# The third batch's attention scores from q and k as loaded (float32), and the order of the whole program searched anew

## The chip, the cores and the metric

The kernel runs on one core of one Trainium2 chip. The metric is the device time of the whole program in microseconds (us), the median of several runs. TensorE (PE in the rows) has the matrix products, VectorE (DVE), ScalarE (ACT) and GpSimd (POOL) the work by element, and SyncE (SP) issues every transfer from one queue, in order.

## The reference

```python
B, H, S, D = 8, 8, 576, 64                       # batches, heads, tokens, width of a head
scores = matmul(q, k.T) / sqrt(D)
cum = cumsum(log(clip(f, 1e-4, 1)), axis=-1)
scores = where(causal, -1e9, scores + cum[:, :, :, None] - cum[:, :, None, :])
attn = softmax(scores)
x = matmul(attn, v)                              # [8 * 576, 512] after the heads are put side by side
h = x @ w_in                                     # [4608, 1024]
solu = h * softmax(h)
ln = (solu - mean(solu)) / sqrt(var(solu) + 1e-6) * g_ln
out = ln @ w_out                                 # [4608, 512]
```

Here q and k are of such a size that rounding them once to 16 bits is too coarse for the result.

## The kernel before

**Attention.** Two heads of a batch make a pair: 32 pairs, four to a batch, pairs 0 to 3 in batch 0. Within a pair the 576 queries are cut into five row blocks, of which block i sees 64 + 128i keys (64, 192, 320, 448 and 576; the last in two pieces of 288). For each piece `score_products` multiplies q by k for both heads, one head on each half of the array's rows (L825), and adds the decay by a product with `pick` or `e8` (L823, L821). VectorE then takes the mask and the row maximum (L846), ScalarE the exponential with its sum (L851), GpSimd and VectorE the reciprocal (L857, L858). The weights of a row block are written as two float16 words (high by ScalarE or GpSimd through the helper lines L507 and L509, low by VectorE, L879), turned by a transposing DMA (L516), and multiplied by v (L928).

**Two ways to the scores.** `NAT` says for how many batches q and k are used as they were loaded. For pairs of batches 0 to NAT - 1, `load` brings q and k straight into one of the four slots `qk16_0` to `qk16_3` (in the rows qk, qk_0_70 to qk_3_73), and L825 is one float32 product for each piece and head. A float32 product is recorded as two weight loads and two matmuls. For the other batches `load` brings them into one of four buffers `raws`. ScalarE then sums their squares (`squares`, L687), a chain of small VectorE and TensorE steps turns the sums into powers of two (`scale`, L640 to L676), and `split_qk` writes each of q and k as a high word (GpSimd, L509) and a low word (VectorE, L780) into the slot. L825 is then three float16 products: high by high, low by high, high by low. v is split in the same way for all batches but the first, so that its squares and its scale exist for every batch.

**The layer.** The 4608 tokens are 36 layers of 128 tokens. Each takes 24 products of 512 columns with w_in (L959 to L961, two words on both sides), the maximum (L970), the exponential (L973), products and sums (L977, L987), the normalisation (L997), two words of the result (L507, L1001), a transposing DMA, and 24 products with w_out (L1029 to L1031). A layer starts when the four pairs of its tokens are done, while later pairs are still under way.

**The order.** Every step is an `op` of a planner, `Plan`. It places the steps on the five engines by a greedy rule, in which the number that a step has in the table `RANK` decides among those that could go next. The engines then run the lists that come out of it, each strictly in its order. `NAT` alters the number of steps (a batch taken as loaded has no squares, no scale and no words of q and k), so that a table belongs to one NAT.

**Filler products.** Where the planner expects TensorE to be idle in the first 300 us, products of `ident` with itself are put into its list (L1154), so that its clock is not lowered. Their number follows from the planner's expectation. Their output is never read.

Of the kernel before, what the change touches and what calls it, by code (L numbers as in the profile page):

```python
# [48 lines left out]
NRAW, NQK, NS, NAT = 4, 4, 6, 2  # L49
# [31 lines left out]
class Plan:  # L81
# [159 lines left out]
    1, 10, 5, 18, 27, 2, 4, 3, 15, 25, 6, 16, 20, 8, 24, 30, 32, 36, 39, 41, 31, 33, 38, 42, 46, 49, 85, 167, 171, 182, 163, 185, 34, 126, 12, 14, 21,  # L241
    28, 7, 22, 11, 40, 9, 29, 13, 56, 59, 62, 67, 72, 77, 17, 97, 90, 105, 109, 114, 127, 132, 143, 23, 26, 35, 44, 48, 177, 191, 47, 55, 58, 64, 70,
    60, 63, 69, 73, 78, 82, 84, 92, 96, 98, 94, 65, 71, 68, 76, 80, 54, 89, 86, 100, 118, 103, 112, 93, 110, 95, 119, 116, 121, 133, 149, 155, 37, 45,
    52, 57, 74, 138, 157, 75, 83, 104, 108, 101, 106, 124, 123, 120, 115, 129, 131, 140, 137, 142, 134, 99, 0, 107, 102, 111, 125, 117, 122, 145, 147,
    141, 159, 139, 144, 130, 136, 169, 172, 175, 184, 188, 50, 66, 79, 87, 91, 195, 206, 113, 151, 150, 146, 148, 153, 154, 156, 158, 161, 165, 168,
    197, 170, 199, 180, 162, 166, 176, 173, 179, 181, 183, 187, 204, 245, 189, 211, 192, 194, 196, 205, 248, 250, 260, 270, 273, 51, 81, 88, 128, 135,
    164, 174, 160, 178, 210, 200, 212, 198, 217, 220, 214, 202, 223, 225, 239, 246, 254, 243, 203, 201, 207, 209, 213, 218, 227, 224, 258, 261, 253,
    262, 233, 256, 234, 237, 263, 267, 269, 277, 279, 190, 230, 216, 240, 296, 259, 193, 247, 231, 257, 272, 265, 244, 278, 382, 390, 293, 300, 266,
    289, 291, 298, 302, 306, 314, 318, 322, 335, 340, 343, 370, 383, 359, 365, 388, 446, 379, 451, 381, 445, 403, 452, 395, 469, 353, 467, 347, 283,
    288, 290, 292, 294, 297, 303, 308, 315, 323, 330, 339, 356, 374, 392, 408, 419, 430, 402, 424, 444, 440, 443, 453, 457, 472, 477, 494, 517, 524,  # L250
    531, 338, 351, 355, 366, 372, 377, 380, 386, 393, 404, 413, 423, 428, 435, 441, 460, 455, 476, 463, 470, 479, 482, 485, 501, 503, 508, 521, 537,
    539, 615, 625, 208, 221, 219, 215, 226, 222, 251, 255, 264, 268, 228, 235, 232, 236, 242, 241, 249, 252, 271, 275, 276, 421, 274, 396, 282, 418,
    280, 407, 286, 400, 320, 325, 334, 341, 238, 299, 281, 284, 285, 287, 295, 313, 319, 316, 304, 309, 307, 311, 317, 321, 326, 329, 333, 331, 324,
    327, 332, 362, 348, 354, 345, 350, 342, 357, 411, 416, 427, 439, 312, 360, 344, 337, 352, 346, 358, 361, 363, 368, 369, 376, 373, 378, 384, 391,
    399, 405, 409, 414, 398, 420, 397, 425, 438, 437, 429, 433, 426, 436, 431, 442, 449, 458, 389, 447, 410, 406, 415, 412, 422, 434, 461, 450, 456,
    462, 459, 465, 468, 475, 483, 490, 493, 506, 471, 474, 480, 492, 528, 526, 448, 515, 514, 520, 549, 565, 579, 581, 590, 597, 599, 603, 611, 632,
    641, 645, 652, 662, 673, 688, 691, 703, 713, 737, 743, 756, 726, 734, 739, 786, 792, 796, 800, 805, 806, 808, 812, 817, 819, 684, 690, 700, 705,
    720, 742, 746, 751, 765, 778, 788, 799, 797, 809, 824, 833, 840, 854, 901, 904, 974, 909, 911, 917, 920, 954, 1028, 967, 229, 305, 367, 454, 301,
    364, 336, 371, 385, 387, 394, 401, 473, 484, 432, 545, 466, 498, 481, 486, 488, 496, 491, 495, 499, 500, 504, 510, 512, 519, 516, 522, 535, 530,
    527, 525, 507, 505, 513, 509, 518, 523, 529, 533, 542, 536, 546, 534, 547, 582, 584, 586, 596, 602, 532, 543, 538, 540, 541, 544, 548, 550, 552,  # L260
    555, 573, 560, 553, 558, 551, 556, 562, 559, 569, 572, 577, 583, 598, 594, 606, 604, 655, 665, 674, 721, 417, 502, 557, 561, 564, 578, 563, 566,
    585, 587, 568, 571, 591, 607, 610, 616, 612, 614, 618, 623, 620, 621, 567, 570, 574, 580, 589, 592, 601, 605, 608, 613, 622, 631, 638, 675, 678,
    694, 706, 709, 576, 617, 593, 588, 600, 595, 609, 619, 624, 627, 630, 637, 633, 642, 629, 636, 654, 649, 657, 667, 679, 671, 699, 683, 663, 729,
    762, 769, 785, 813, 464, 497, 628, 635, 639, 650, 640, 647, 664, 666, 656, 670, 677, 681, 686, 701, 685, 687, 693, 704, 689, 695, 644, 646, 660,
    658, 668, 682, 702, 708, 692, 712, 696, 714, 724, 775, 777, 779, 791, 801, 648, 710, 669, 659, 676, 680, 697, 707, 718, 715, 753, 750, 717, 723,
    719, 725, 727, 759, 757, 787, 793, 790, 807, 804, 770, 811, 828, 844, 888, 892, 478, 511, 716, 731, 732, 736, 730, 733, 741, 755, 738, 747, 760,
    764, 767, 789, 766, 772, 784, 795, 774, 781, 748, 744, 752, 749, 758, 763, 773, 768, 780, 776, 794, 802, 783, 821, 822, 823, 829, 834, 754, 816,
    798, 810, 803, 814, 835, 845, 848, 851, 853, 857, 827, 832, 825, 830, 837, 842, 871, 890, 893, 902, 907, 910, 864, 914, 965, 972, 1007, 1011, 152,
    489, 349, 487, 839, 855, 859, 862, 867, 870, 878, 883, 898, 906, 912, 922, 923, 929, 941, 950, 962, 973, 1030, 1033, 1038, 1046, 1050, 1120, 1127,
    1145, 1160, 1164, 925, 928, 930, 935, 939, 945, 948, 951, 959, 968, 976, 986, 988, 998, 1025, 1032, 1040, 1051, 1100, 1105, 1110, 1126, 1149,  # L270
    1151, 1174, 1179, 1187, 1193, 985, 990, 997, 1005, 1012, 1014, 1017, 1020, 1029, 1036, 1047, 1062, 1054, 1085, 1129, 1152, 1172, 1184, 1218, 1225,
    1108, 1230, 1242, 1248, 1255, 1264, 1271, 1279, 1055, 1059, 1065, 1072, 1075, 1078, 1082, 1087, 1095, 1102, 1121, 1135, 1128, 1142, 1161, 1169,
    1220, 1231, 1273, 1286, 1292, 1297, 1307, 1320, 1336, 1341, 1349, 1382, 1137, 1141, 1162, 1166, 1182, 1186, 1204, 1206, 1221, 1224, 1238, 1252,
    1247, 1269, 1284, 1301, 1331, 1353, 1409, 1412, 1420, 1423, 1428, 1431, 1433, 1443, 1448, 1452, 43, 61, 53, 19, 575, 186, 328, 634, 310, 375, 643,
    651, 653, 661, 672, 698, 885, 897, 728, 820, 745, 818, 761, 949, 979, 836, 882, 841, 846, 849, 850, 863, 856, 858, 869, 872, 894, 891, 874, 877,
    896, 895, 886, 880, 843, 847, 860, 866, 881, 889, 980, 899, 937, 952, 1042, 900, 955, 963, 964, 983, 1016, 1026, 852, 969, 868, 873, 875, 887,
    903, 908, 916, 919, 957, 977, 924, 931, 921, 926, 936, 915, 960, 970, 981, 978, 994, 1018, 987, 1023, 1093, 1097, 1101, 1103, 771, 876, 722, 815,
    782, 1015, 933, 958, 942, 944, 943, 946, 956, 961, 947, 953, 984, 989, 996, 999, 1004, 1000, 993, 1001, 1003, 1006, 966, 971, 1009, 1019, 1031,
    1037, 1064, 1048, 1077, 1071, 1021, 1013, 1081, 1111, 1113, 1115, 1117, 1125, 992, 1024, 1008, 1002, 1034, 1027, 1049, 1056, 1061, 1057, 1119,
    1092, 1035, 1039, 1041, 1044, 1045, 1060, 1098, 1099, 1107, 1122, 1148, 1150, 1124, 1155, 1188, 1194, 1203, 1254, 740, 861, 735, 838, 913, 1022,  # L280
    1043, 1053, 1066, 1068, 1063, 1067, 1073, 1074, 1076, 1079, 1104, 1106, 1118, 1114, 1112, 1116, 1133, 1083, 1130, 1132, 1086, 1091, 1090, 1096,
    1139, 1144, 1156, 1158, 1159, 1183, 1146, 1136, 1196, 1235, 1237, 1240, 1244, 1250, 1131, 1153, 1140, 1138, 1157, 1143, 1168, 1173, 1185, 1201,
    1189, 1215, 1165, 1170, 1163, 1167, 1175, 1181, 1207, 1213, 1233, 1243, 1263, 1259, 1222, 1267, 1268, 1313, 1323, 1344, 831, 927, 865, 934, 1010,
    1080, 1171, 1200, 1177, 1180, 1176, 1178, 1195, 1197, 1190, 1192, 1202, 1214, 1216, 1226, 1217, 1223, 1256, 1228, 1227, 1246, 1208, 1210, 1211,
    1219, 1232, 1245, 1265, 1260, 1280, 1283, 1261, 1251, 1288, 1325, 1328, 1330, 1338, 1342, 1212, 1258, 1229, 1234, 1236, 1241, 1249, 1253, 1262,
    1257, 1303, 1266, 1270, 1274, 1272, 1276, 1277, 1281, 1294, 1300, 1358, 1310, 1367, 1348, 1306, 1387, 1456, 1461, 1494, 1497, 1346, 1357, 1363,
# [912 lines left out]
```

## Time and profile before

| | us |
|---|---|
| median of 3 runs | 665.16 (665.11 to 666.92) |
| the profiled execution, its own time | 663.76 |
| its span, from the first to the last instruction | 661.9 |
| TensorE busy in it | 633.3 |
| VectorE busy in it | 558.0 |
| ScalarE busy in it | 519.7 |
| GpSimd busy in it | 403.0 |

The span lies within the execution's own time; 1.9 us are outside. The own time is 1.4 us under the median. "Busy" is the time in which an engine has at least one instruction under way. Matmuls overlap and their ends are modelled, so the distance from one start to the next says more than a duration. An idle time carries the name of what ended it. A wait for several things is put down to the one that came last. The mean granted TensorE clock was 0.997 of its full 2.4 GHz.

### The profile page before, as it was taken

What the parts mean: (1) busy time and instruction counts of PE and PEld (TensorE: products, weight loads), DVE (VectorE), ACT (ScalarE), POOL (GpSimd) and SP (SyncE); (2) the same over time, 40 slices, a digit from 0 to 9 for tenths busy, and PEclk for the clock granted to TensorE, in tenths of its full rate; (3) what the DMA queues carried; (4) which work ended last, traced back from release to release, by engine and by line L of the source; (5) the groups of instructions that cost most, each with busy time, mean ns of one, the idle gap of its engine ahead of it and who ended that gap; (6) DMA issues with size and microseconds to landing.
All of it is one profiled execution on the core that took longest, in us unless ns stands there. A gap on an engine that the chain in (4) does not pass through costs nothing. (4 is left out here: it accounts for less than half of the span.)

```text
span 661.9 us, 17333 instructions
## 1 busy us (share of the span) xinstructions
PE 633.3 (96%) x6304; PEld 343.2 (52%) x6304; DVE 558.0 (84%) x1640; ACT 519.7 (79%) x1294; POOL 403.0 (61%) x625
## 2 busy tenths in 40 slices
PE   6899999999999999999999999999998999999998
PEld 4655655655554546454454555445544544544445
DVE  6777999999998999999989998889899977884222
ACT  6999938978979989898796996998786869655432
POOL 4465851386767845887578666765776645556440
PEclk9999999999999999999999999999999999999999
DMA  8856118879889997999899898699657984877341
GB/s 340 315 187 227 41 37 231 143 128 225 173 174 191 189 213 145 170 246 202 197 166 197 157 226 201 151 195 190 136 117 136 156 155 83 160 133 141 78 96 48
DMA packets 262709, 110.79 MB, mean 167 GB/s; under 512 B 248288, under 2 KB 248736, under 8 KB 261600
## 3 DMA queue, kind: packets, MB, share of 16 engines
q1 hardware_dynamic: 262624, 109.69, 77.1%
q8 instruction: 49, 0.80, 0.5%
q14 instruction: 36, 0.29, 0.1%
HBM read 38.27 MB, written 9.66 MB: 72 GB/s over the span
## 5 line engine op out<-in xcount | busy, mean ns | idle before, releaser
L851 ACT ACTIVATE p<-p,nm 128x448 f32<-128x448 f32 (+4 forms) x208 | 132.9, 641 | 25.7 <-DVE nm L846 25.3
L825 PE MATMUL ps<-qk 64*128 64x288 f16 (+9 forms) x1056 | 103.3, 306 | 8.6 <-DMA qk<-in_qk_dram 4.9
L959 PE MATMUL hps<-wi_h,x_h 128*128 128x512 f16 x288 | 109.6, 381 | 1.8 <-DVE e L977 1.8
L961 PE MATMUL hps<-wi_h,x_l 128*128 128x512 f16 x288 | 109.1, 379 | 0.0
L960 PE MATMUL hps<-wi_l,x_h 128*128 128x512 f16 x288 | 109.1, 379 | 0.0
L1029 PE MATMUL ps<-wo_f,zz 128*128 128x512 f16 x280 | 106.6, 381 | 2.4 <-DVE p16s L879 1.3
L857 POOL TENSOR_SCALAR sm<-sm 128x2 f32<-128x2 f32 (+1 forms) x128 | 38.5, 301 | 111.7 <-ACT p L851 83.1
L1031 PE MATMUL ps<-wo_f,zz 128*128 128x512 f16 x280 | 106.1, 379 | 0.0
L1030 PE MATMUL ps<-wo_f,zz 128*128 128x512 f16 x280 | 106.1, 379 | 0.0
L846 DVE CUSTOM_DVE_ANT_0 p<-ps,mask 128x448 f32<-128x448 f32 (+4 forms) x208 | 97.6, 497 | 5.8 <-PE ps L823 3.0
L879 DVE SCALAR_TENSOR_TENSOR wo_p<-p,ri,wo_p 128x448 f16<-128x448 f32 (+1 forms) x112 | 96.5, 880 | 3.7 <-ACT wo_p L507 2.6
L1001 POOL TENSOR_TENSOR z<-e,z 128x1024 f16<-128x1024 f32 x32 | 71.6, 2239 | 21.6 <-ACT z L507 21.2
L928 PE MATMUL ps<-t_p,v 128*64 128x128 f16 (+1 forms) x2520 | 80.7, 219 | 3.1 <-DVE nm L846 1.5
L928 PEld LDWEIGHTS <-v 128*64 128x64 f16 x2520 | 70.8, 110 | 24.7 <-issue 22.6
L970 DVE TENSOR_REDUCE st<-hps 128x1 f32<-128x1024 f32 x36 | 43.7, 1214 | 28.6 <-PE hps L961 28.6
L509 POOL TENSOR_SCALAR wo_p<-p,ri 128x576 f16<-128x576 f32 x56 | 52.9, 952 | 14.9 <-DVE ri L858 10.1
L973 ACT ACTIVATE e<-hps,st,unscale 128x1024 f32<-128x1024 f32 x32 | 38.4, 1201 | 25.0 <-DVE st L971 19.9
L823 PE MATMUL ps<-crow,pick 64*128 64x448 bf16 (+1 forms) x360 | 51.7, 276 | 0.0
L977 DVE SCALAR_TENSOR_TENSOR e<-hps,e 128x1024 f32<-128x1024 f32 x36 | 43.8, 1217 | 9.3 <-ACT e L973 8.8
L825 PEld LDWEIGHTS <-qk 64*128 64x128 f16 x864 | 32.3, 94 | 37.0 <-issue 26.1
L997 POOL TENSOR_SCALAR e<-e,st 128x1024 f32<-128x1024 f32 x32 | 47.4, 1483 | 2.9
L509 POOL TENSOR_SCALAR qk<-raws,scale 128x576 f16<-128x576 f32 x48 | 40.3, 844 | 14.6 <-DVE scale L676 8.3
(188 smaller groups left out, 1300.4 us busy)
## 6 DMA issues: line engine op xcount, KB each, us to landing
raws<-in_qk_dram SPq DMA_DIRECT2D x24, 576.0 KB, 4.8
vraw<-in_v_dram SPq DMA_DIRECT2D x8, 1280.0 KB, 6.7
out_dram<-y SPq DMA_DIRECT2D x35, 256.0 KB, 2.8
qk<-in_qk_dram SPq DMA_DIRECT2D x8, 576.0 KB, 7.9
wo_raw<-in_w_in_dram SPq DMA_DIRECT2D x4, 1024.0 KB, 7.9
t_raw<-in_w_out_dram SPq DMA_DIRECT2D x2, 1024.0 KB, 4.8
vraw<-in_w_out_dram SPq DMA_DIRECT2D x2, 1024.0 KB, 6.2
t_p<-p16s SPq DMA_TRANSPOSE x84, 3.4
```

Of the source, the lines that this page charges most:

```text
L509: (nc.vector if eng == DVE else nc.gpsimd).tensor_scalar(now(out_), now(in_), scale, by, ALU.mult, ALU.mult)
L825: nc.tensor.matmul(dst, x[row(h), 0, q0:q0 + P], y[row(h), 1, cols], start=(n == 0), stop=False)
L846: op(DVE, R_NS[i] if n == 0 else 442, at[i][h] + STEPS[0], lambda i=i, h=h, n=n, a=a, e=e, x=x, m0=m0: nc.vector.tensor_tensor_reduce(home ...
L851: op(ACT, E_NS[i] + (0 if banked(p, i) or i == 4 else 28), at[i][h] + STEPS[1], lambda i=i, h=h, x=x: nc.scalar.activation(home(i, h), hom ...
L879: op(DVE, L_NS[j], at[j][g] + STEPS[4], lambda j=j, g=g, nq=nq, h16=h16, l16=l16, r1=r1: nc.vector.scalar_tensor_tensor(l16(), home(j, g, ...
L928: nc.tensor.matmul(o[row(h), a:a + n], v16[m][:, x, 2 * j + h], t[:, y, i + j if h else i - j], start=(j == 0 and c == 0), stop=(j == i an ...
L959: nc.tensor.matmul(hps[:, sl], x_h, wi_h[:, c, sl], start=(c == 0), stop=False)
L960: nc.tensor.matmul(hps[:, sl], x_h, wi_l[:, c, sl], start=False, stop=False)
L961: nc.tensor.matmul(hps[:, sl], x_l, wi_h[:, c, sl], start=False, stop=(c == NCC - 1))
L1029: nc.tensor.matmul(o, zz[:, a, 0, j], wo(0, k), start=(k == 0), stop=False)
L1030: nc.tensor.matmul(o, zz[:, a, 0, j], wo(1, k), start=False, stop=False)
L1031: nc.tensor.matmul(o, zz[:, a, 1, j], wo(0, k), start=False, stop=(k == NFC - 1))
```

## The change

`NAT` goes from 2 to 3, and `RANK` is another table. Batch 2 (pairs 8 to 11) now takes q and k as loaded: its eight `split_qk` steps on GpSimd and its eight on VectorE are gone, as are its four sums of squares of q and k. Its `scale` is that of v alone: one column to turn instead of three, and five small VectorE steps fewer. Its loads go into the slots `qk16` and not into `raws`. L825 of these four pairs is one float32 product for each piece and head where it was three float16 products. `pick` holds a factor for them of 8 where it was 128, since q and k no longer carry one. Everything else differs only in its order.

```diff
-NRAW, NQK, NS, NAT = 4, 4, 6, 2
+NRAW, NQK, NS, NAT = 4, 4, 6, 3
 RANK = (
-    1, 10, 5, 18, 27, 2, 4, 3, 15, 25, 6, 16, 20, 8, 24, 30, 32, 36, 39, 41, 31, 33, 38, 42, 46, 49, 85, 167, 171, 182, 163, 185, 34, 126, 12, 14, 21,
...
```

The table has one line fewer, so that every line of the changed kernel stands one lower: L825 is L824 there.

What the table does is seen in the lists of the engines. The first place is on TensorE, at the first piece of pair 8's scores (block 0, 64 keys; qk_0_70 is slot 0, ps_145 and ps_148 are the banks of the two heads). Before:

```order
L928 MATMUL ps_150<-t_0_p,v_2_81 64x128
L825 LDWEIGHTS qk_0_70
L825 MATMUL ps_145<-qk_0_70 128x64
L825 LDWEIGHTS qk_0_70
L825 MATMUL ps_148<-qk_0_70 128x64
...
L823 LDWEIGHTS pick
L823 MATMUL ps_145<-crow,pick 128x64
L823 LDWEIGHTS pick
L823 MATMUL ps_148<-crow,pick 128x64
L825 LDWEIGHTS qk_0_70
L825 MATMUL ps_145<-qk_0_70 128x192
```

And in the changed kernel:

```order
L927 MATMUL ps_150<-t_1_p,v_3_82 64x128
L824 MATMUL ps_145<-qk_0_70 128x64
L824 MATMUL ps_148<-qk_0_70 128x64
L822 LDWEIGHTS pick
L822 MATMUL ps_145<-crow,pick 128x64
L822 LDWEIGHTS pick
L822 MATMUL ps_148<-crow,pick 128x64
L824 MATMUL ps_145<-qk_0_70 128x192
```

Six products and their loads have become two float32 products, which the list shows as one row each, and they stand behind the products of pair 7 with v where they stood behind those of pair 6. Over the whole list of TensorE there are 130 fillers before and 95 now: 41 and 36 ahead of the first score product, 70 and 51 between it and the first product of a layer (L959), 19 and 8 behind that. A place where a score piece, a product with v or a full 128x128 product or transpose is followed by one of another of these three kinds occurs 295 times before and 279 times now.

The second place is on VectorE, at the last row maximum of pair 7 (p_67 and nm_88 are its block 4). Before:

```order
L846 ISA p_66,nm_88<-ps_148,mask 128x448
L846 ISA nm_88 128x1
L939 SCALAR_TENSOR_TENSOR x_l<-ps_147,x_h 128x256
L780 SCALAR_TENSOR_TENSOR qk_1_71<-raws,scale_119,qk_1_71 128x576
L780 SCALAR_TENSOR_TENSOR qk_0_70<-raws,scale_119,qk_0_70 128x576 x2
L846 ISA p_67,nm_88<-ps_148,mask 128x288
```

And in the changed kernel:

```order
L938 SCALAR_TENSOR_TENSOR x_l<-ps_147,x_h 128x256
L857 RECIPROCAL ri_92<-sm_96 128x2
L878 SCALAR_TENSOR_TENSOR wo_p_1244<-p_67,ri_91,wo_p_1244 128x576
L938 SCALAR_TENSOR_TENSOR x_l<-ps_150,x_h 128x320
L845 ISA p_67,nm_88<-ps_148,mask 128x288
```

The three low words of batch 2 that stood ahead of this maximum are gone, and work of pairs 6 and 7 stands there. On ScalarE the exponential of the second layer (L973, L972 now) is row 97 of the list before and row 87 now.

The third place is on SyncE, at the first transposes of pair 4 (t_0_p) and pair 5 (t_1_p). Before:

```order
L516 DMA_TRANSPOSE t_0_p<-p16s_83 128x10x128
L513 DMA vraw_77<-in_v_dram 128x4x640
L513 DMA out_dram<-y_142 128x512
L513 DMA vraw_76<-in_v_dram 128x4x640
L516 DMA_TRANSPOSE t_0_p<-wo_p_1267 128x14x128
L516 DMA_TRANSPOSE t_0_p<-wo_p_1267 128x18x128
L516 DMA_TRANSPOSE t_1_p<-p16s_84 128x2x64
```

And in the changed kernel:

```order
L515 DMA_TRANSPOSE t_0_p<-p16s_83 128x10x128
L512 DMA qk_0_70<-in_qk_dram 128x1152
L512 DMA vraw_76<-in_v_dram 128x4x640
L515 DMA_TRANSPOSE t_0_p<-wo_p_1244 128x14x128
L512 DMA out_dram<-y_142 128x512
L515 DMA_TRANSPOSE t_0_p<-wo_p_1244 128x18x128
L515 DMA_TRANSPOSE t_1_p<-p16s_84 128x10x128
L515 DMA_TRANSPOSE t_1_p<-p16s_84 128x2x64
L512 DMA qk_1_71<-in_qk_dram 128x1152
```

The loads of batch 2 into the slots stand among the transposes of batch 1; the four loads into `raws` at the start are there before and after, but bring batch 3 now.

## Rows read from the trace of the kernel before

**Rows 1.** The page's first part: busy time, share of the span and instructions of each engine.

```profile
PE 633.3 (96%) x6304; PEld 343.2 (52%) x6304; DVE 558.0 (84%) x1640; ACT 519.7 (79%) x1294; POOL 403.0 (61%) x625
```

**Rows 2.** Busy time by stage: stretch, its length, then busy time and count of instructions of TensorE, its weight loads, VectorE, ScalarE and GpSimd, the granted clock of TensorE (1.00 is full speed), the share of the DMA engines and GB/s.

```profile
20.00:60.00 40.00, 35.79 (x338) 23.54 (x340) 28.79 (x96) 38.10 (x102) 24.05 (x47) 1.00 0.61 221
60.00:100.00 40.00, 38.98 (x312) 23.72 (x311) 38.16 (x112) 29.75 (x72) 25.31 (x46) 1.00 0.23 79
100.00:400.00 300.00, 292.30 (x3158) 154.72 (x3156) 286.04 (x871) 258.75 (x666) 200.08 (x287) 1.00 0.93 187
400.00:600.00 200.00, 194.07 (x2025) 100.84 (x2020) 172.90 (x505) 155.99 (x397) 123.34 (x182) 1.00 0.78 151
```

**Rows 3.** Who ended TensorE's idle time between 100 and 600 us: the waiting engine, tile and line, what it waited for, us in total, times, the longest.

```profile
PE hps L959 <- DVE e L977: 1.8, 3, 1.1
PE ps L928 <- DVE nm L846: 1.5, 2, 0.9
PE ps L670 <- DVE scale L668: 1.4, 2, 1.2
PE ps L825 <- DVE x_l L939: 1.3, 1, 1.3
PE ps L1029 <- DVE p16s L879: 1.3, 2, 0.7
PE ps L825 <- DVE nm L846: 1.1, 2, 0.9
PE ps L1154 <- DVE x_l L939: 1.0, 1, 1.0
```

**Rows 4.** Score pieces of batch 1, taken as loaded, on TensorE in order of time: start us, duration, engine, line, operation, tiles, shapes and type, count.

```profile
105.81 0.44 PE L825 MATMUL ps<-qk 64*128 64x64 f32 x4
...
107.40 1.31 PE L923 MATMUL ps<-t_p,vraw 128*64 128x128 f32 x20
108.64 1.02 PE L825 MATMUL ps<-qk 64*128 64x448 f32 x4
...
109.78 1.12 PE L928 MATMUL ps<-t_p,v 128*64 128x64 f16 x36
...
146.61 0.76 PE L825 MATMUL ps<-qk 64*128 64x288 f32 x4
...
148.02 1.79 PE L928 MATMUL ps<-t_p,v 128*64 128x64 f16 x60
```

**Rows 5.** Score pieces of batch 2, split into words, on TensorE, with the same columns.

```profile
149.75 0.26 PE L825 MATMUL ps<-qk 64*128 64x64 f16 x6
...
150.84 0.39 PE L959 MATMUL hps<-wi_h,x_h 128*128 128x512 f16 x1
...
152.56 0.74 PE L825 MATMUL ps<-qk 64*128 64x448 f16 x6
...
153.42 0.39 PE L959 MATMUL hps<-wi_h,x_h 128*128 128x512 f16 x1
...
180.45 0.38 PE L960 MATMUL hps<-wi_l,x_h 128*128 128x512 f16 x1
180.67 0.38 PE L961 MATMUL hps<-wi_h,x_l 128*128 128x512 f16 x1
180.98 0.54 PE L825 MATMUL ps<-qk 64*128 64x288 f16 x6
...
182.06 0.39 PE L1029 MATMUL ps<-wo_f,zz 128*128 128x512 f16 x1
```

**Rows 6.** Groups of instructions by line, with shapes kept apart: line, engine, operation, tiles, shapes, count, then busy us, mean ns of one, idle us before them and what ended it.

```profile
L780 DVE SCALAR_TENSOR_TENSOR qk<-raws,scale,qk 128x576 f16<-128x576 f32 x48 | 47.1, 1001 | 0.0
L509 POOL TENSOR_SCALAR qk<-raws,scale 128x576 f16<-128x576 f32 x48 | 40.3, 844 | 14.6 <-DVE scale L676 8.3 <-PE ps L825 5.3
L825 PEld LDWEIGHTS <-qk 64*128 64x128 f16 x864 | 32.3, 94 | 37.0 <-issue 26.1 <-POOL st L991 0.8 <-DVE p16s L879 0.8
L687 ACT ACTIVATE junk<-raws 128x1152 bf16<-128x1152 f32 x24 | 27.8, 1158 | 1.5 <-DMA raws<-in_qk_dram 1.3
L825 PEld LDWEIGHTS ps<-qk 64*128 64x128 f32 x192 | 15.9, 194 | 14.4 <-DMA qk<-in_qk_dram 5.2 <-DVE nm L846 3.4 <-issue 1.8
L687 ACT ACTIVATION_READ_ACCUMULATOR junk<-raws 128x1 f32 x24 | 4.6, 192 | 0.0
L645 PE MATMUL ps<-ident,top 128*1 128x128 f32 x20 | 3.5, 272 | 0.0
L664 DVE TENSOR_SCALAR scale<-scale 1x1 f32<-1x1 f32 x6 | 1.2, 201 | 0.2
```

**Rows 7.** Two stretches of filler products on TensorE, with the product behind each, in order of time.

```profile
17.66 1.80 PE L1154 MATMUL hps<-ident 128*128 128x256 bf16 x15
19.60 0.38 PE L670 MATMUL ps<-scale_wi,ones 1*128 1x2 f32 x2
...
122.38 1.69 PE L1154 MATMUL ps<-ident 128*128 128x256 bf16 x14 [0.25 <-DVE nm L846]
124.00 1.03 PE L928 MATMUL ps<-t_p,v 128*64 128x128 f16 x30
```

**Rows 8.** What the transfer queue of SyncE waited for: the line, what it waited for, us in total, times, the longest.

```profile
SPq L513 <- PE ps L823: 33.6, 4, 14.9
SPq L516 <- PE ps L823: 18.1, 12, 3.1
```

288 rows, old and new, of the table RANK are left out of this document.

## The prediction

> **What bounds the kernel now.** I read the busy times first. TensorE is busy for 96% of the span and VectorE for 84% [rows 1], so the end can come sooner only if TensorE's list gets shorter or waits less. By stage [rows 2] there are two parts. From 20 to 60 us ScalarE is the full engine, 38.1 of 40 us, while TensorE idles for 4.2 us and runs fillers besides. From 100 to 400 us TensorE (292.3 of 300) and VectorE (286.0) are both nearly full. From 400 to 600 us VectorE has room (172.9 of 200), and TensorE still idles for 5.9 us. The granted clock is full in all of them, so no time hangs on the clock there.
>
> Next, who ends TensorE's idle time. Between 100 and 600 us it is 500 - 292.3 - 194.1 = 13.6 us, and the seven longest entries [rows 3], all with VectorE's name, make 9.4 us of it. So two things decide: how much longer TensorE's own work becomes, and how much of the 13.6 us goes when VectorE has less to do.
>
> **TensorE: the float32 products.** The price is read from start to start, over pieces of the same columns, the product with `pick` included. The blocks of 64, 192 and 320 keys: 105.81 to 107.40 as loaded, 1.59 us [rows 4], 149.75 to 150.84 in words, 1.09 us [rows 5]; 0.50 more. The block of 448: 108.64 to 109.78 is 1.14 us against 152.56 to 153.42, 0.86 us; 0.28 more. Two pieces of 288: 146.61 to 148.02 is 1.41 us against 180.98 to 182.06, 1.08 us; 0.33 more. That is 1.11 us for a pair, 4.4 us for four. A part of it is the weight load, which takes 194 ns in float32 and 94 ns in float16 [rows 6].
>
> The Trainium skill ("FP8 and Floating Point Precision", TensorE Precision Notes) counts a true float32 product as four passes through the array, against the three products in words here. One pass more over the 1,600 columns of a pair, at the 0.22 us between starts of a 512-column product [rows 5], would be 0.7 us a pair and 2.7 us in all, an estimate. The trace has 4.4 us, and its rows decide.
>
> **TensorE: what becomes less.** Two transposes of sums are gone. Each takes at most its mean of 272 ns [rows 6], back to back less; I take 0.3 us for both. The list has 16 changes of kind fewer (279 for 295). A change costs what 180.67 to 180.98 has over 180.45 to 180.67 [rows 5], 0.31 - 0.22 = 0.09 us, so they give 1.4 us. The work that has to be done therefore grows by 4.4 - 0.3 - 1.4 = 2.7 us.
>
> **The fillers.** There are 35 fewer. One costs (19.60 - 17.66) / 15 = 0.13 us, or (124.00 - 122.38) / 14 = 0.12 us [rows 7]. A filler fills a wait, and its absence pays only if the wait gets shorter too. The five at the start stand ahead of the first load's landing and are worth nothing. The 19 up to the first layer are worth 0 to 2.3 us; they lie where ScalarE is full, and its list now reaches the second layer's exponential ten rows earlier. I take half, 1.2 us. The 11 behind that are worth 0 to 1.3 us. The 14 of rows 7 lay by batch 2's chain of scales, which gets shorter, so I take 1.0 us. Together 2.2 us.
>
> **The other engines.** VectorE loses eight low words at 1.00 us, 8.0 us, and five small steps of at most 0.20 us [rows 6]: 9.0 us. ScalarE loses four sums of squares of 1.158 + 0.192 us, 5.4 us, and GpSimd eight high words of 0.844 us, 6.8 us. None of it shortens the end directly, since TensorE's list has to run anyway. It matters by the waits it shortens: a VectorE that is 95% full from 100 to 400 us is up to 9.0 us ahead behind batch 2, and what TensorE waited for in rows 3 is done sooner. The bounds are 0 (TensorE and VectorE go in step, and new waits take the place of the old) and the whole 9.4 us. I take 4.5 us, nearly half: several of these are waits for a row maximum or a low word that is itself one step of a chain through ScalarE and GpSimd, and a static list with four slots and six banks can't carry all of a lead on.
>
> **The moved transfers.** The loads of pairs 8 to 11 now wait until a slot is free, among the transposes of batch 1, so that those behind them wait too. The four loads of this kind for batch 1 waited 33.6 us in all, where little stood behind them; transposes that waited for TensorE's scores took 18.1 / 12 = 1.5 us [rows 8]. The new loads stand behind a transpose of the same pair, whose scores are mostly done, so 1.5 us is nearer than 8.4. A transpose that is 1.5 us late is covered as long as TensorE has layers in hand, which it has from the first layers on. I take 0, with 4 x 1.5 = 6 us if that cover is gone. Bytes moved don't change.
>
> **The sum.** 2.7 - 2.2 - 4.5 = -4.0 us. On the profiled execution's own time that is 663.76 - 4.0 = 659.8; the median of the runs stands 1.4 us above it, so I forecast 665.2 - 4.0 = 661.2 us. A difference of 0.3%, 2.0 us, is about what a measurement of this kernel can tell from no change.
>
> **The rivals.**
>
> *The float32 passes are paid in full.* TensorE is 96% busy, so 4.1 us of longer products (4.4 - 0.3) may come straight on top, with the lists' other gains: 2.7 us if the 16 changes of kind pay and neither the idle time nor the fillers' waits get shorter, 665.2 + 2.7 = 667.9. For it speaks that VectorE and TensorE are full at once, and that each reordering brings waits of its own. Against it speaks that nearly all of TensorE's long waits carry VectorE's name. It decides when less than 0.7 us of waits and fillers is won back, since 2.7 - 0.7 is the limit of 2.0. I give it 0.19.
>
> *A wash.* Waits and fillers give back about what the products cost, 2.7 us of the 6.7 that I count: 665.2, from 663.2 to 667.2. The idle time of TensorE is spread over many small waits, and a wait that VectorE ends may be ended next by ScalarE. I give it 0.20.
>
> *VectorE is the real bound.* Then its relief comes through: all of the 9.4 us goes, and the fillers' 3.6 us in full, 2.7 - 9.4 - 3.6 = -10.3, 654.9 us. For it speaks its 95% from 100 to 400 us, against it that it is 86% busy from 400 to 600, where TensorE idles just as often. I give it 0.07. The Trainium skill ("Perfetto Trace Analysis", Identifying the Most-Contended Engine) points this way: it takes occupancy as a fair measure for VectorE and says that matmul busy time is none for TensorE. The trace bears it out in part, since TensorE waits for VectorE, but for 13.6 us of 500 only.
>
> *The loads block the transposes.* The 6 us above appear in full: -4.0 + 6.0 = +2.0, 667.2. I give it 0.04.
>
> **How the numbers follow.** The forecast itself has 0.50, from 657.5 to 663.2: its lower end has all of the fillers and 7 us of waits. Faster is the forecast and the third rival, 0.57. Same is the wash, 0.20. Slower is the first and the fourth, 0.23. The range for 8 in 10 leaves out most of the third rival below and the far end of the first above: 656.5 to 668.0.
>
> **What would show it.** In the changed profile VectorE's busy time falls by some 9 us, ScalarE's by 5.4 and GpSimd's by 6.8. A pair of batch 2 takes 1.1 us longer in its score pieces. If I am right, TensorE's idle time between 100 and 600 us falls from 13.6 us to about 9, and the entries with VectorE's name shrink. If TensorE idles as before there, or if new waits for ScalarE or for a transposing DMA appear, the first two rivals hold. I would be wrong above all in the 4.5 us, which is a share taken between two bounds, and in the waits of the new order, which no row of before can show.

## The result, and the profile of the changed kernel

The changed kernel takes 670.78 us (median of 4 runs, 669.87 to 671.89), the kernel before, measured with it, 666.04 us (a fourth run of it moved this median up from the 665.16 us that the forecast starts from). The ratio is 1.0068, with a 95% interval of 1.0042 to 1.0093: slower by 4.7 us, where 661.2 us was forecast. Its profiled execution took 671.53 us, with a span of 669.8 us. The profiled execution of before took 663.76 us, 2.3 under its median here, and that of the changed kernel lies 0.8 over its own, so that some 3 of the 7.9 us between the two spans lie in the choice of executions. Sizes are taken from the medians where both exist.

Line numbers are one lower than before. First the busy line of the page, then busy time by stage, with the columns of [rows 1, 2]:

```profile
PE 633.7 (95%) x6219; PEld 342.2 (51%) x6219; DVE 544.6 (81%) x1627; ACT 511.2 (76%) x1286; POOL 388.8 (58%) x617
```

```profile
20.00:60.00 40.00, 36.01 (x330) 22.51 (x325) 29.58 (x102) 37.47 (x101) 26.40 (x49) 1.00 0.59 223
100.00:400.00 300.00, 289.44 (x3020) 153.29 (x3021) 270.08 (x847) 249.73 (x649) 184.36 (x278) 1.00 0.91 182
400.00:600.00 200.00, 191.12 (x2039) 99.53 (x2038) 173.54 (x507) 153.44 (x398) 120.54 (x180) 0.98 0.77 149
525.00:530.00 5.00, 5.00 (x31) 1.87 (x28) 3.95 (x16) 3.96 (x17) 1.68 (x5) 0.66 0.84 156
550.00:555.00 5.00, 3.04 (x10) 1.21 (x11) 4.45 (x15) 4.18 (x10) 1.46 (x6) 0.81 0.77 105
555.00:560.00 5.00, 5.00 (x21) 2.15 (x20) 0.45 (x4) 0.96 (x3) 1.71 (x2) 0.85 0.35 67
```

VectorE is relieved by 13.4 us, ScalarE by 8.5 and GpSimd by 14.2, more than the forecast's 9.0, 5.4 and 6.8. But from 100 to 600 us TensorE idles for 500 - 289.4 - 191.1 = 19.4 us, where it idled for 13.6 [rows 2] and about 9 was forecast. The last three rows show the granted clock of TensorE under 1.00 at 525 us and again at 550; it was 1.00 in every stage of [rows 2]. Who ended TensorE's idle time from 100 to 600 us, as in [rows 3]:

```profile
PE ps L1028 <- DMA zz<-z: 4.9, 4, 2.4
PE ps L824 <- DVE nm L845: 3.2, 3, 2.1
PE hps L958 <- DVE e L976: 2.4, 2, 1.7
PE ps L927 <- DVE nm L845: 1.8, 1, 1.8
```

Before, no single wait in this stretch was longer than 1.3 us [rows 3]. Now there are two of 2.1 and 2.4 us, and three of 1.6 to 1.8.

To see where time goes, a ruler that all kernels share: every layer but the last has 48 products of 512 columns (L958 to L960 and L1028 to L1030), and mark n is the start of the product with the number 48n + 1; the last column is the end of the span. The table has it in us for before, and the difference from it for the others. The two orders lay attention work differently between the layers, so that marks in the middle sway: f9_words, with no wait over 1 us between marks 20 and 24, goes from -1.9 to +4.5 there. Across the two orders the end tells, and the early marks roughly; between kernels of one order every mark does.

```
mark (us before)    0 (55.4)  3 (141.3)  8 (222.7)  20 (425.3)  24 (489.5)  28 (558.7)  end (661.9)
changed kernel        -3.8       -4.3       +1.1       -0.9        +5.6       +12.6       +7.9
f1_products           +0.8       +0.7       +5.8       +6.0        +6.0        +7.2       +7.1
f2_old_order          +0.3       +3.7       +8.2      +11.4       +13.4       +13.4      +13.0
f6_relief             +0.7       +0.5       +4.5       +5.3        +6.7        +7.3       +7.2
f3_wait1              -3.9       -3.6       +2.0       -0.1        +5.8        +7.9       +3.4
f5_both               -3.9       -4.1       +1.6       -0.4        +6.0        +7.1       +2.4
f9_words              -3.1       -3.4       +2.1       -1.9        +4.5        +5.7       +1.0
```

The changed kernel is best read against f5_both (below), which has its order but for three steps. Up to mark 24 the two differ by 0.5 us or less; at mark 28 the changed kernel is 5.5 us behind, and it stays 5.5 behind to the end. These 5.5 us are lost in the last batches, whose work the change does not touch.

### The profile page after: what moved, and what is told of

Read it like the earlier page. It is cut to its first block, busy times and chain, and to the rows that moved or that the text cites. A ratio compares the mean times of both kernels' runs of the same rounds, so it can differ in the third digit from the quotient of the medians.

```text
span 669.8 us, 17156 instructions
## 1 busy us (share of the span) xinstructions
PE 633.7 (95%) x6219; PEld 342.2 (51%) x6219; DVE 544.6 (81%) x1627; ACT 511.2 (76%) x1286; POOL 388.8 (58%) x617
## 5 line engine op out<-in xcount | busy, mean ns | idle before, releaser
L824 PE MATMUL ps<-qk 64*128 64x288 f16 (+9 forms) x1008 | 106.9, 321 | 10.2 <-DMA qk<-in_qk_dram 4.6
L1028 PE MATMUL ps<-wo_f,zz 128*128 128x512 f16 x280 | 107.8, 385 | 7.3 <-DMA zz<-z 4.9
L958 PE MATMUL hps<-wi_h,x_h 128*128 128x512 f16 x288 | 109.8, 381 | 2.4 <-DVE e L976 2.4
L856 POOL TENSOR_SCALAR sm<-sm 128x2 f32<-128x2 f32 (+1 forms) x128 | 39.9, 312 | 122.2 <-ACT p L850 86.3
L960 PE MATMUL hps<-wi_h,x_l 128*128 128x512 f16 x288 | 109.4, 380 | 0.0
L959 PE MATMUL hps<-wi_l,x_h 128*128 128x512 f16 x288 | 109.4, 380 | 0.0
L1029 PE MATMUL ps<-wo_f,zz 128*128 128x512 f16 x280 | 107.2, 383 | 0.0
L1030 PE MATMUL ps<-wo_f,zz 128*128 128x512 f16 x280 | 107.1, 383 | 0.0
L878 DVE SCALAR_TENSOR_TENSOR wo_p<-p,ri,wo_p 128x576 f16<-128x576 f32 (+1 forms) x112 | 94.0, 859 | 3.2 <-ACT wo_p L506 2.5
L1000 POOL TENSOR_TENSOR z<-e,z 128x1024 f16<-128x1024 f32 x32 | 69.3, 2167 | 29.5 <-ACT z L506 29.0
L972 ACT ACTIVATE e<-hps,st,unscale 128x1024 f32<-128x1024 f32 x32 | 38.4, 1201 | 27.8 <-DVE st L970 20.7
L508 POOL TENSOR_SCALAR wo_p<-p,ri 128x576 f16<-128x576 f32 x56 | 46.5, 835 | 16.0 <-DVE ri L857 13.0
L976 DVE SCALAR_TENSOR_TENSOR e<-hps,e 128x1024 f32<-128x1024 f32 x36 | 43.9, 1219 | 13.6 <-ACT e L972 13.5
L986 ACT ACTIVATE junk<-e,st 128x1024 bf16<-128x1024 f32 x36 | 41.2, 1144 | 10.8 <-DVE e L976 10.6
L1028 PEld LDWEIGHTS <-zz 128*128 128x128 f16 x280 | 27.5, 98 | 41.8 <-DMA zz<-z 8.0
L958 PEld LDWEIGHTS <-x_h 128*128 128x128 f16 x288 | 28.1, 97 | 38.6 <-issue 10.3
```

What stands on the lines that cost most here:

```text
L824: nc.tensor.matmul(dst, x[row(h), 0, q0:q0 + P], y[row(h), 1, cols], start=(n == 0), stop=False)
L878: op(DVE, L_NS[j], at[j][g] + STEPS[4], lambda j=j, g=g, nq=nq, h16=h16, l16=l16, r1=r1: nc.vector.scalar_tensor_tensor(l16(), home(j, g, ...
L958: nc.tensor.matmul(hps[:, sl], x_h, wi_h[:, c, sl], start=(c == 0), stop=False)
L959: nc.tensor.matmul(hps[:, sl], x_h, wi_l[:, c, sl], start=False, stop=False)
L960: nc.tensor.matmul(hps[:, sl], x_l, wi_h[:, c, sl], start=False, stop=(c == NCC - 1))
L1000: op(Z_LO[n], {DVE: 1280, POOL: 2130}[Z_LO[n]], at, lambda: engine(Z_LO[n]).tensor_tensor(z16[:, :, 1], e2, z16[:, :, 0], ALU.subtract), [ ...
```

## The two long waits

**The first, at 522 us.** VectorE, GpSimd and TensorE in the changed kernel, each in order of time (start, duration, engine, line, operation, tiles, shapes, count, in brackets the idle time before it and what ended it):

```profile
519.54 0.45 DVE L845 CUSTOM_DVE_ANT_0 p<-ps,mask 128x288 f32<-128x288 f32 x1
519.91 2.50 DVE L878 SCALAR_TENSOR_TENSOR wo_p<-p,ri,wo_p 128x448 f16<-128x448 f32 x1
522.34 1.03 DVE L878 SCALAR_TENSOR_TENSOR p16s<-p,ri,p16s 128x320 f16<-128x320 f32 x1
523.29 0.67 DVE L878 SCALAR_TENSOR_TENSOR wo_p<-p,ri,wo_p 128x448 f16<-128x448 f32 x1
523.89 0.51 DVE L845 CUSTOM_DVE_ANT_0 p<-ps,mask,nm 128x288 f32<-128x288 f32 x1
...
519.81 2.13 POOL L1000 TENSOR_TENSOR z<-e,z 128x1024 f16<-128x1024 f32 x1 [1.24 <-ACT z L506]
...
522.01 0.30 PE L824 MATMUL ps<-qk 64*128 64x320 f16 x1
524.45 0.56 PE L824 MATMUL ps<-qk 64*128 64x320 f16 x5 [2.14 <-DVE nm L845]
526.08 0.63 PE L959 MATMUL hps<-wi_l,x_h 128*128 128x512 f16 x1
526.51 0.63 PE L960 MATMUL hps<-wi_h,x_l 128*128 128x512 f16 x1
...
529.07 0.47 PE L1030 MATMUL ps<-wo_f,zz 128*128 128x512 f16 x1
```

Three low words stand ahead of the maximum that frees the bank. The first of them takes 2.50 us, its twin two rows on 0.67 us: it begins 0.1 us after GpSimd's L1000 and ends 0.5 us after it. TensorE waits 2.14 us for the maximum, and then eight products of 512 columns start 0.43 us apart (526.08 to 529.07) where 0.22 is usual. That is the lower of the two levels, 1.2 GHz, and costs at least 1.5 us more.

**The second, at 549 us.** SyncE's queue, GpSimd, VectorE and TensorE:

```profile
536.20 7.83 SPq L515 DMA_TRANSPOSE t_p<-p16s  x5
544.13 0.68 SPq L512 DMA_DIRECT2D out_dram<-y  x1
544.90 3.57 SPq L515 DMA_TRANSPOSE zz<-z  x1
...
539.86 2.88 POOL L1000 TENSOR_TENSOR z<-e,z 128x1024 f16<-128x1024 f32 x1 [1.35 <-ACT z L506]
...
539.93 0.80 DVE L779 SCALAR_TENSOR_TENSOR qk<-raws,scale,qk 128x576 f16<-128x576 f32 x1
...
551.96 0.39 PE L1028 MATMUL ps<-wo_f,zz 128*128 128x512 f16 x1 [2.44 <-DMA zz<-z]
553.39 0.63 PE L1028 MATMUL ps<-wo_f,zz 128*128 128x512 f16 x1
553.82 0.63 PE L1029 MATMUL ps<-wo_f,zz 128*128 128x512 f16 x1
```

z is ready when L1000 ends at 542.74, but its transpose stands behind five others and a store, and is issued at 544.90. L1000 itself is late: it takes 2.88 us where 2.13 is usual, and its excess of 0.75 us is about the time for which VectorE's L779 ran beside its start. So there it was GpSimd that was held. TensorE waits 2.44 us, and its starts are 0.43 us apart again (553.39 to 553.82).

## The experiments

**f1_products: the products alone, in the order of before.**

```
-            passes = ((x32, x32),) if p < NAT * NPAIR else ((hi, hi), (lo, hi), (hi, lo))
+            passes = ((x32, x32),) if p < 3 * NPAIR else ((hi, hi), (lo, hi), (hi, lo))
```

> The kernel before, its order, its splits, its squares and every wait kept; only the products of batch 2's scores are one float32 product on the bits that lie in the slots, where they were three float16 products. What is multiplied is meaningless, and the output is left out of account. Theory A (the float32 products are paid in full, since TensorE's list has no room that would take them in): 666.0 + 4 x 1.11 = 670.4 us. Rival (TensorE's waits behind batch 2 get shorter by as much): 666 to 667 us.

Measured: 670.72 us (670.59 to 671.22), ratio 1.0064 (1.0039 to 1.0089), 4.6 us over before. The price worked out from the pieces, 4.4 us, is paid in full, and on the ruler it is paid where batch 2's scores lie, between marks 3 and 8.

**f2_old_order: the change, with the places in the order that its steps had before.** NAT is 3, and RANK is that of before with the entries of the steps that are gone passed over.

```
-        o.due = RANK[o.seq]
+        o.due = RANK[o.seq + self.passed]
...
+        plan.passed += 4 if p // NPAIR == 2 else 0
...
+            plan.passed += 2 if b == 2 else 0
```

> The change without a new search: NAT = 3, and each step that is left keeps the number that it had in the table of before. Beside the first experiment it has the relief of VectorE (9.0 us), ScalarE and GpSimd, and no new table. Theory A (the relief buys next to nothing, since no wait of TensorE hangs on the sum of VectorE's work): 668.5 to 670.5 us. Rival (the prediction's term, 4.5 us of waits won back): 666.0 + 4.4 - 0.3 - 4.5 = 665.6 us.

Measured: 676.64 us (676.22 to 680.12), ratio 1.0163 (1.0127 to 1.0198), 10.6 us over before. Neither expectation held. With the relief, but with places that were searched for other work, the kernel is 6 us worse than with the products alone. Its trace has 156 fillers where before has 130, and two long waits, of 1.91 us at 119 and 2.12 us at 304, with the granted clock down behind each (0.81 from 118 to 124 us, 0.66 from 305 to 310). So the old places did not suit the new work, and this run changes too much at once to give a price of the relief.

**f6_relief: f1_products with the relief, in the order of before.** In `squares` and `split_qk`:

```
+        if b == 2 and j:
+            src, dst = src[:, :, :1], dst[:, :, :1]
...
+            if b == 2:
+                plan.ops[-1].fn = lambda: None
```

> f6_relief is f1_products (the old order, batch 2's scores by one float32 product instead of three float16 ones) with the split of batch 2's q and k left out (32 instructions of 0.8 to 1.0 us on VectorE, GpSimd and ScalarE) and its squares cut to one column (4 instructions of 1.16 us on ScalarE become 0.2). The products of batch 2 so read what batch 1 left in the slots, and its output is meaningless; the order, and everything else, is that of f1_products. Theory A (the relief falls into slack, TensorE waits for other things): 669.5 to 671, no more than 1.2 under f1_products' 670.7. Theory P (the prediction's term: half of VectorE's relief of 9.0 us comes back as shorter waits of TensorE): 666.2. Anything between: the term had the right sign, and its size is what is measured.

The edit takes out 16 instructions, eight on VectorE and eight on GpSimd, not the 32 of the expectation. Measured: 672.78 us (671.11 to 674.1), ratio 1.0102 (1.0072 to 1.0131), with a median above f1_products' by 2.1 us; the spans of the two profiled executions are 669.1 and 669.0 us. The first part of each page, f1_products and then f6_relief, and two rows of what TensorE waited for from 100 to 600 us, of f6_relief (its lines stand six higher than those of before: L934 is L928 there, L1035 is L1029):

```profile
PE 638.1 (95%) x6256; PEld 345.9 (52%) x6256; DVE 563.2 (84%) x1640; ACT 519.4 (78%) x1294; POOL 402.0 (60%) x625
```

```profile
PE 637.2 (95%) x6256; PEld 344.7 (52%) x6256; DVE 555.7 (83%) x1632; ACT 516.4 (77%) x1294; POOL 393.1 (59%) x617
```

```profile
PE ps L934 <- DMA t_p<-p16s: 2.6, 4, 1.5
...
PE ps L1035 <- DMA zz<-z: 1.4, 2, 1.2
```

VectorE has 7.5 us less to do, GpSimd 8.9, and nothing of it reaches the end: from 100 to 600 us TensorE idles for 15.9 us, in f1_products for 15.7. On the ruler the lead over f1_products is 1.3 us at mark 8, where the words were, 0.7 at mark 20, and gone by mark 24; between marks 20 and 24 TensorE waits for transposes, the 1.2 us one for zz among them. Theory P, 666.2, falls. Theory A is borne out in what it says, that in this order the relief falls into slack; its range, 669.5 to 671, was missed by the median. The three runs above the profiled one show a mean granted clock of 0.992 where it shows 0.995, and have no trace.

**f3_wait1 and f5_both: the changed kernel without its two long waits.** Behind the planner a step is put ahead of another in the order (the words behind # here and below are explanations):

```
+        for x in (3023, 3025):      # the two maxima of pair 27 that free the banks
+            ahead(x, 3020)          # ahead of the first of the three low words
+        ahead(2715, 3208)           # f5_both alone: the transpose of zz ahead of the last of the five
```

> The changed kernel, with two row maxima of pair 27 put ahead of three low words on VectorE's list; nothing else is moved. TensorE waited 2.14 us at 522 us for the banks that these maxima free, and its clock fell behind that wait (eight products of 0.43 us where 0.22 is usual, 1.7 us). Theory A (the new order's late waits and the clock behind them make the change slower): 670.8 - 2.1 - 1.7 = 667.0 us. Rival (another wait takes its place): 669.5 to 671 us.

> The changed kernel with the edit of the third experiment and, on SyncE's list, the transpose of layer 26 put ahead of one transpose of pair 28 and of an output store. TensorE waited 2.44 us for that transpose at 549 us, and its clock fell behind the wait, 1.7 us more. Theory A: 670.8 - 3.8 - 4.1 = 662.9 us, faster than the kernel before. Rival (the products are what costs, and other waits take the place of these two): 667 to 671 us.

Measured: f3_wait1 666.57 us (665.13 to 669.81), ratio 1.0010 (0.9992 to 1.0028), 4.2 us under the changed kernel, as expected. f5_both 665.90 us (664.88 to 666.79), ratio 0.9993 (0.9978 to 1.0008); it was expected at 662.9, and gains only 0.7 us more, which is not clear of noise. In f3_wait1 the second wait was down to 1.73 us, with the clock at 1.00 behind it, so that less was left to take. VectorE and GpSimd in f3_wait1 at the place of the first wait, then TensorE at that of the second:

```profile
520.34 0.52 DVE L845 CUSTOM_DVE_ANT_0 p<-ps,mask,nm 128x288 f32<-128x288 f32 x1
520.79 0.51 DVE L845 CUSTOM_DVE_ANT_0 p<-ps,mask,nm 128x288 f32<-128x288 f32 x1
521.22 1.41 DVE L878 SCALAR_TENSOR_TENSOR wo_p<-p,ri,wo_p 128x448 f16<-128x448 f32 x1
...
520.02 2.14 POOL L1000 TENSOR_TENSOR z<-e,z 128x1024 f16<-128x1024 f32 x1 [1.24 <-ACT z L506]
...
549.36 0.39 PE L1028 MATMUL ps<-wo_f,zz 128*128 128x512 f16 x1 [1.73 <-DVE p16s L878]
```

Its busy time from 550 to 560 us, with the clock behind the five engines:

```profile
550.00:560.00 10.00, 10.00 (x114) 5.35 (x113) 6.17 (x16) 7.80 (x19) 5.44 (x9) 1.00 0.36 83
```

The maxima run at their usual pace beside L1000 (520.02 to 522.16). The low word behind them starts inside it and is done 0.5 us after L1000 is.

**f7_waits: four more places changed by hand.**

```
+        behind(3004, 2687)          # a transpose of p16s behind that of zz, before 531 us
+        ahead(1887, 1679)           # maxima of pair 16 ahead of a low word, 291 us
+        ahead(1886, 1679)
+        ahead(1768, 2042)           # L976 ahead of a low word, 346 us
+        ahead(1747, 2044)           # the transpose of zz ahead of one of p16s, 349 us
```

> f7_waits is f5_both with four more places of the new order changed, each one step put ahead of, or behind, its neighbours on its engine: the block maxima that free the banks at 294 us ahead of a low word that GpSimd holds up, the second pass over the hidden layer at 346 us (L976) ahead of one low word, the transpose of zz at 349 us ahead of one of the p16s, and the transpose of zz before 531 us ahead of one of the p16s. Theory A (the new order's loss is a handful of long waits of TensorE, each its own): waits of 1.83, 1.69, 1.64 and 1.58 us are cut by 1.3, 0.9, 1.0 and 1.0 us, and the time falls by 3 to 4 us from f5_both's 665.9 to 662 to 663, under the kernel before (666.1). Theory B (a removed wait is taken up by the next one): 665 to 666, with waits of about the same size a few us further on.

In this kernel the two maxima of pair 16 also came ahead of their own scores and are taken of what the bank held; the instructions are the same. Measured: 667.14 us (665.81 to 668.4), ratio 1.0005 (0.9991 to 1.0019), 1.2 us over f5_both instead of 3 to 4 under it. One move made a wait of its own. VectorE, GpSimd and TensorE around 346 us, first f5_both, then f7_waits, and busy time and clock of f7_waits behind the wait:

```profile
345.44 0.95 DVE L878 SCALAR_TENSOR_TENSOR p16s<-p,ri,p16s 128x320 f16<-128x320 f32 x1
346.32 1.21 DVE L976 SCALAR_TENSOR_TENSOR e<-hps,e 128x1024 f32<-128x1024 f32 x1
...
346.48 2.13 POOL L1000 TENSOR_TENSOR z<-e,z 128x1024 f16<-128x1024 f32 x1 [0.42 <-ACT z L506]
```

```profile
346.23 2.37 DVE L878 SCALAR_TENSOR_TENSOR p16s<-p,ri,p16s 128x320 f16<-128x320 f32 x1
...
348.79 0.46 DVE L938 SCALAR_TENSOR_TENSOR x_l<-ps,x_h 128x320 f16<-128x320 f32 x1
...
346.12 2.13 POOL L1000 TENSOR_TENSOR z<-e,z 128x1024 f16<-128x1024 f32 x1 [0.42 <-ACT z L506]
...
349.30 0.90 PE L824 MATMUL ps<-qk 64*128 64x288 f16 x6 [2.13 <-DVE x_l L938]
```

```profile
350.00:355.00 5.00, 5.00 (x21) 2.00 (x18) 4.44 (x13) 4.65 (x10) 4.81 (x5) 0.50 1.19 169
```

The same low word takes 0.95 us where it begins before L1000 and 2.37 us where it begins 0.1 us into it. L938 behind it is late, TensorE waits 2.13 us, and the clock stands at 0.50, 1.2 GHz, for the next 5 us. This is the first wait of the changed kernel over again, made by a move. The wait at 531 us went, but 1.24 us came back at 543 us, for a word of x that VectorE and ScalarE brought no sooner.

**f9_words: the held words put where nothing waits behind them.** f5_both and:

```
+        ahead(1887, 1364)           # maxima of pair 16 behind their scores, ahead of L969
+        ahead(1886, 1364)
+        behind(1679, 1364)          # the held low word behind L969
+        ahead(1768, 2042)           # L976 and L938 ahead of the low word
+        behind(2042, 2032)
+        behind(2046, 1747)          # its transpose behind that of zz
```

> f9_words is f5_both with two more stretches of the new order changed, chosen by what f7_waits showed (a low word on VectorE, L878 from p, whose start falls into GpSimd's L1000 lasts until L1000 ends: 0.95 us became 2.37). Around 291 us the block maxima of pair 16 go ahead of the low word that GpSimd holds (2.55 us) and of the reduction L969. Around 346 us the second pass over the hidden layer (L976) and the low word of x (L938) go ahead of one low word from p, which then waits out L1000 with nothing that TensorE needs behind it, and the transpose of zz goes ahead of that word's. Theory A (TensorE waits for what stands behind a held word, and the clock stays up): the waits of 1.83, 1.69 and 1.64 us shrink by 1.0 us or more each, no stretch falls under a granted clock of 0.95 after 20 us, and the time is 662 to 664. Theory B (VectorE and ScalarE are late there as a whole, so that a wait taken away comes back within some 20 us, as the one at 531 us came back at 543 us): 665 to 666, as f5_both's 665.9.

Measured: 663.57 us (662.99 to 664.75), ratio 0.9958 (0.9941 to 0.9974): faster by 2.7 us than the kernel before, which took 666.27 us beside it. It is 7.2 us under the changed kernel's 670.78, but that was not measured on the same chip. VectorE and GpSimd around 346 us, what TensorE waited for longest from 100 to 600 us, two rows of busy time, and the first part of the page:

```profile
346.21 0.46 DVE L938 SCALAR_TENSOR_TENSOR x_l<-ps,x_h 128x320 f16<-128x320 f32 x1
...
346.79 1.53 DVE L878 SCALAR_TENSOR_TENSOR p16s<-p,ri,p16s 128x320 f16<-128x320 f32 x1
...
345.84 2.13 POOL L1000 TENSOR_TENSOR z<-e,z 128x1024 f16<-128x1024 f32 x1 [0.43 <-ACT z L506]
```

```profile
PE ps L1028 <- DMA zz<-z: 2.7, 2, 1.6
PE hps L958 <- DVE e L976: 1.5, 2, 0.8
```

```profile
20.00:660.00 640.00, 620.45 (x6142) 333.57 (x6140) 529.65 (x1598) 497.73 (x1262) 382.01 (x588) 1.00 0.78 162
100.00:600.00 500.00, 485.70 (x5099) 255.68 (x5096) 446.99 (x1365) 407.41 (x1056) 309.79 (x464) 1.00 0.87 171
```

```profile
PE 633.0 (95%) x6219; PEld 342.3 (52%) x6219; DVE 543.0 (82%) x1627; ACT 511.4 (77%) x1286; POOL 388.4 (59%) x617
```

The word still outlasts L1000 (345.84 + 2.13), by 0.35 us, but L938 is ahead of it now, inside L1000, at its usual 0.46 us. The wait of 1.83 us at 294 us is gone, those of 1.69 and 1.64 at 346 and 354 us are down to 0.8 and 1.1: 0.9 and 0.5 less, where theory A named 1.0 or more each. The clock holds, and the time of theory A, 662 to 664, came true.

## Why the prediction was wrong

**Right: the products.** 1.11 us a pair, 4.4 us in all, was forecast, and f1_products measures 4.6. The pieces themselves, in the changed kernel on TensorE (two of 288 keys of batch 2, with the product with `pick`, and what follows):

```profile
161.86 0.76 PE L824 MATMUL ps<-qk 64*128 64x288 f32 x4
...
162.58 0.65 PE L824 MATMUL ps<-qk 64*128 64x288 f32 x4
...
163.28 0.39 PE L958 MATMUL hps<-wi_h,x_h 128*128 128x512 f16 x1
```

From 161.86 to 163.28 is 1.42 us, as for batch 1 [rows 4] and 0.34 more than in words [rows 5], where 0.33 was worked out. The estimate from four passes, 2.7 us, falls.

**Wrong in size, on the safe side: the fillers.** 2.2 us were counted for all of them, 1.2 of it up to the first layer. By mark 3 the new order is 5.0 us ahead of the same products in the old one (-4.3 against +0.7), though a part of that may be attention work laid elsewhere. The busy times say the same without the ruler: f9_words' TensorE is busy for 633.0 us and f1_products' for 638.1, with the same mean granted clock, 0.83, in the first 20 us. These 5.1 us are about what 35 fillers at 0.12 us, 4.2 us, and the changes of kind would give if both were paid nearly in full.

**Wrong: the 4.5 us of waits won back by VectorE's relief.** This is the step that failed. f6_relief gives the relief alone in the old order, and it is worth nothing at the end. In the new order TensorE's idle time from 100 to 600 us was to fall from 13.6 us to about 9. It is 19.4 us in the changed kernel, and still 14.3 in f9_words, without the two long waits and without a fall of the clock, against 15.7 in f1_products. So the best order tried wins back some 1.4 us of the 4.5. The step took the waits named after VectorE for a share of its load. The rows of the long ones show single instructions that stand behind others in a list that is fixed beforehand; that this goes for the many short ones too is argued, not shown.

**Missing: waits that the new order makes.** They stood at nothing in the sum. The forecast gave the fillers, the transposes, the changes of kind and the waits together 2.2 + 0.3 + 1.4 + 4.5 = 8.4 us against the products. From f1_products to the changed kernel, 670.72 to 670.78, none of it is left. Moving three steps (f5_both) brings 4.9 us back: the waits of 2.14 and 2.44 us and the clock's fall behind each, between 490 and 560 us. Moving six more, at 291 and 346 us (f9_words), brings 2.3 more. That ends 7.2 us under f1_products, near the 8.4 by number, but not by the forecast's way: of the 6.1 us between the two spans (669.0 and 662.9) 5.1 are the busy time above, and 1.0 is idle time. The prediction named this source of error, since no row of before can show the new order's waits, but its range ended at the sum of costs that did show, 668.0.

**The rivals.** "The float32 passes are paid in full" comes nearest, and its words that each reordering brings waits of its own name the cause; its 667.9 has no long wait and no fall of the clock in it. "A wash" ended at 667.2, under every run of the changed kernel. "VectorE is the real bound" falls with f6_relief. "The loads block the transposes" is not seen: from 100 to 300 us, where the new loads stand, TensorE waits for a transpose once, for 0.2 us. The sign that was named for the first two rivals, new waits for a transposing DMA, did come, with 4.9 us for zz.

**Open.** f3_wait1 took the clock's first fall away together with its wait, so the two have no separate price beyond the rows. Why VectorE and GpSimd are relieved by more than was counted is only known in part: 14 low words were held by an L1000 before, 9 in the changed kernel. Why a part of the wait at 531 us came back at 543 us is read from one trace alone. Whether moves of this kind would help the order of before too was not tried.

## What to carry to other kernels

A longer product on an engine that is 96% busy costs its length, read from start to start; relief of the engine beside it paid nothing where the order was fixed (f6_relief). When a fixed order is made anew, look in its trace for the few longest waits before judging the change: nine moved steps turned a loss of 4.7 us into a gain of 2.7, though the gain forecast, 4.0, was not reached. Put a VectorE instruction that can be held by GpSimd behind those that free a bank, not ahead of them.

## What the runs showed of the hardware

A VectorE word of two inputs in SBUF (L878 from p and the high word) that begins while GpSimd's L1000 runs ends only after it: 2.50 us instead of 0.67, 2.37 instead of 0.95. In the traces of all nine kernels 100 such words (L878 from p, and L779, by the lines of the changed kernel) begin inside an L1000, and 96 end 0.34 to 0.74 us after it. The other four are L779 in kernels of the new order, as at 539.93 above: VectorE's word before it was still under way when L1000 began, L779 took its usual 0.80 us, and it was L1000 that took 2.82 to 2.88 us instead of 2.13. So here the one that came first went on, and the other was held, whichever engine it was. Instructions with one of their inputs in a bank of PSUM are not held: beside L1000 the maxima took 0.51 us and L938 0.46. The Trainium skill ("GPSIMD Engine Reference", 1. Specifications) says that GpSimd shares its SBUF interfaces with VectorE and contends with VectorE instructions that have two SBUF inputs; these rows agree, and the sum of the prediction had no place for it.

TensorE's granted clock fell to 1.2 GHz after the waits of 2.13, 2.14 and 2.44 us quoted above, in f7_waits as soon as work began again and in the changed kernel both times a little over 1 us later, and cost 1.5 us or more each time. It fell behind those of 1.91 and 2.12 us in f2_old_order too; behind the wait of 1.73 us in f3_wait1 and that of 1.83 in the changed kernel it stayed at 1.00.
